# Cluster one-hots on GpSimd and ScalarE, mask rows by transfers, and another order of preparation in an attention and MoE kernel

## The chip, the cores and the metric

The kernel runs on one core of a Trainium2 chip. The metric is the device time of one execution in microseconds (us). TensorE (PE in the profile) multiplies and transposes; VectorE (DVE), ScalarE (ACT) and GpSimd (POOL) compute; SyncE (SP) and GpSimd issue the transfers. Each engine runs its instructions in the order in which the program gives them, and a waiting instruction holds up all behind it.

## What is computed

Clustered attention (2 batches, 8 heads, 768 positions, 64 features), then two MoE layers on its 1536 x 512 result. The change lies in the attention alone.

```python
q_assign = np.argmax(np.einsum('bhsd,hcd->bhsc', q_n, c_n), axis=-1)   # 16 clusters a head
k_assign = np.argmax(np.einsum('bhsd,hcd->bhsc', k_n, c_n), axis=-1)
mask = q_assign[:, :, :, None] == k_assign[:, :, None, :]
scores = np.where(mask, scale * np.matmul(q, k.transpose(0, 1, 3, 2)), -1000000000.0)
attn = np.exp(scores - np.max(scores, axis=-1, keepdims=True))
attn = attn / (np.sum(attn, axis=-1, keepdims=True) + 1e-09)
# x = attn @ v, then a gated MoE (512 -> 1536 -> 512) and a 4-expert MoE (512 -> 1024 -> 512)
```

## The kernel before

**Heads and slots.** There are 16 head instances g (2 batches x 8 heads). A unit u is half of a head's queries (384 rows), a slot is 128 query rows, so a unit has 3 slots, a head 6, and a pair of heads (p) 12; 96 slots in all, preceded by 5 slots of lead. The program is in an order written out by hand. In each slot the engines get, in the order "ESTLAtVMlvZB" (L549): the exponential of one score tile (E, `s_exp`, ScalarE), the score matmuls of the tile five slots ahead (S, `s_mm`, TensorE), three transposes of the probabilities (T, `transp`), with a copy "hi" by ScalarE (L347), VectorE's subtraction "lo" for the previous one (L, `low`, L361), the tasks of position a, the value matmuls (V, `pv`), three more transposes (t), the row maximum (M, `s_max`, L324, VectorE), then l, v, and the tasks of positions z and b. So "-9b" in a list of steps means: the last place of the ninth slot before a base slot.

**Scores with a mask.** A score tile is two products summed in PSUM: `t1` (hi and low halves of q and k, 128 rows) and `t2` (64 rows of the other combination, and in rows 64 to 79 the one-hot of the query's cluster and, for the keys, (one-hot - 1) x 2^60). A key of another cluster so gets a huge negative score. Each is done as two halves of 384 keys, in two banks of PSUM (L315 to L319).

**Clusters.** `cluster(g)` (L244) is a generator whose steps are spread over slots: 12 matmuls against the centroids (L259), a ScalarE copy and a VectorE addition (L266, L268), the maximum over 16 clusters (L270), equality with the maximum (L272), a product with tie weights (L274), a second maximum (L275), the one-hot (L277), six TensorE transposes (L283), and four ScalarE operations that write 16 rows of `t2` (L298, L300). Head 0 has its own form (L287 to L290). The lists CL, CL1, CL2 and CL4 (L518 to L521) place the steps.

**Operands.** `load_qk(g)` (L211) brings `t1` and `t2` by GpSimd's queue and the raw halves by SP's; `rest_qk(g)` subtracts the low halves on GpSimd (L226). Heads 0 and 1 come instead by `load_raw`, with the casts `hi_raw`, `hi_t2` and the subtraction `low_raw` by ScalarE and VectorE. `load_v`, `rest_v` (L240, GpSimd) bring the values.

**Pairs.** `recip(p)` makes the reciprocals of the row sums and spreads them by SP transfers: rT to DRAM (`rd`, L415), then R (L418). `pv_out` copies the result and, at the end of a pair, issues three SP transfers x (L394 to L396). `norm(p)` scales on GpSimd (L427, L432, L438) with ScalarE copies (L436).

Of the kernel before, what the change touches and what calls it, by code (L numbers as in the profile page):

```python
# [18 lines left out]
NCL = 16  # L19
# [7 lines left out]
BIG = float(2.0 ** 60)  # L27
F64_LO = 2.0 ** -126
# [7 lines left out]
def tile_cluster_attention_moe(ctx, tc, qk, vt, cent, consts, wm1, wm2, probs, out):  # L36
# [137 lines left out]
    def attention():  # L174
        with ExitStack() as ax:
# [27 lines left out]
            def low_raw(g, j):  # L203
                r = slice(64, 128) if j == 0 else slice(0, 64)
                t = ops[g]["t1"][r, j]
                V.tensor_tensor(out=t, in0=ops[g]["raw"][j][r], in1=t.bitcast(F32), op=ALU.subtract)
# [37 lines left out]
            def cluster(g):  # L244


                N = 2 * NQ
                t1, t2 = ops[g]["t1"], ops[g]["t2"]
                oh = oh_t[g % 2]
                ohn = oh[:, :, :, :NCL]  # L250
                pc = (ps_v if g == 1 else ps_c).tile([128, N, 2, NCL], F32, tag="v" if g == 1 else "c", name="pc")
                sc = clp.tile([128, N, NCL], F32, tag="sc", name="sc", bufs=2)
                mx = clp.tile([128, N, 1], F32, tag="mx", name="mx", bufs=2)
                eq = clp.tile([128, N, NCL], BF16, tag="eq", name="eq", bufs=2)
                mw = clp.tile([128, N, 1], BF16, tag="mw", name="mw", bufs=2)
                wb = wtie.rearrange("p (o c) -> p o c", o=1).to_broadcast([128, N, NCL])
                for j in range(2):
                    for c in range(NQ):
                        T.matmul(  # L259
                            out=pc[:, 2 * c + j].rearrange("p a b -> p (a b)"),  # L260
                            lhsT=t1[:, j, c * 128:(c + 1) * 128],
                            rhs=cT[:, g % H].rearrange("p a b -> p (a b)"),
                            start=True, stop=True,
                        )
                    yield
                A.copy(out=sc, in_=pc[:, :, 1])  # L266
                yield
                V.tensor_tensor(out=sc, in0=pc[:, :, 0], in1=sc, op=ALU.add)  # L268
                yield
                V.tensor_reduce(out=mx, in_=sc, axis=AX.X, op=ALU.max)  # L270
                yield
                V.tensor_tensor(out=eq, in0=sc, in1=mx.to_broadcast([128, N, NCL]), op=ALU.is_equal)  # L272
                yield
                V.tensor_tensor(out=eq, in0=eq, in1=wb, op=ALU.mult)  # L274
                V.tensor_reduce(out=mw, in_=eq, axis=AX.X, op=ALU.max)  # L275
                yield
                V.tensor_tensor(  # L277
                    out=ohn, in0=eq.rearrange("p (c j) n -> p c j n", j=2),
                    in1=mw.rearrange("p (c j) n -> p c j n", j=2).to_broadcast([128, NQ, 2, NCL]), op=ALU.is_equal)
                yield  # L280
                pt = ps_t.tile([64, S], BF16, tag="t", name="pt") if g == 0 else ps_c.tile([64, S], BF16, tag="c", name="pt")
                for c in range(NQ):
                    T.transpose(pt[:, c * 128:(c + 1) * 128], oh[:, c].rearrange("p j n -> p (j n)"), identb)  # L283
                yield
                if g == 0:
                    hs = [slice(i * 384, (i + 1) * 384) for i in range(2)]
                    A.activation(out=t2[64:80, 1, hs[0]], in_=pt[32:48, hs[0]], func=ACTF.Copy, scale=BIG, bias=-BIG)  # L287
                    V.tensor_scalar(out=t2[64:80, 1, hs[1]], in0=pt[32:48, hs[1]], scalar1=1.0, scalar2=BIG, op0=ALU.subtract, op1=ALU.mult)
                    for i in range(2):
                        A.copy(out=t2[64:80, 0, hs[i]], in_=pt[0:16, hs[i]])  # L290
                    yield
                else:
                    for j in range(2):
                        for i in range(2):
                            hs = slice(i * 384, (i + 1) * 384)
                            dst, src = t2[64:80, j, hs], pt[j * 32:j * 32 + 16, hs]
                            if j == 0:
                                A.copy(out=dst, in_=src)  # L298
                            else:
                                A.activation(out=dst, in_=src, func=ACTF.Copy, scale=BIG, bias=-BIG)  # L300
                            yield
# [7 lines left out]
            def s_mm(n):  # L309
# [5 lines left out]
                for c in range(2):  # L315
                    ps = S_t[n][:, c, :384]
                    ks = slice(c * 384, (c + 1) * 384)
# [3 lines left out]
            def s_max(n):  # L321
# [3 lines left out]
                    out=junk.rearrange("p (c n) -> p c n", c=2), in0=S_t[n][:, :, :384],  # L325
                    in1=zero1.rearrange("p (o n) -> p o n", o=1).to_broadcast([128, 2, 384]), scale=-0.125, scalar=3.0e38,
                    op0=ALU.add, op1=ALU.min, accum_out=nm)

            def s_exp(n):
# [6 lines left out]
                A.activation(out=P_t[n].rearrange("p (c n) -> p c n", c=2), in_=S_t.pop(n)[:, :, :384], func=ACTF.Exp, scale=0.125, bias=nm_t.pop(n),  # L336
# [126 lines left out]
            V.memset(zero1, 0.0)  # L463

# [10 lines left out]
            load_raw(1)  # L475
            setup, head = consts_setup(clp, ps_c), cluster(0)
# [3 lines left out]
            hi_raw(0, 0, A.copy)  # L480
            next(setup)
            low_raw(0, 0)
# [5 lines left out]
            low_raw(0, 1)  # L488
# [4 lines left out]
            load_qk(2)  # L493
# [3 lines left out]
            for j in range(2):  # L497
                hi_raw(1, j, A.copy)
            for _ in range(5):
                next(head)  # L500
            warm(8)
            low_raw(1, 0)
            next(head)
            next(head)
            low_raw(1, 1)
            for j in range(2):
                hi_t2(1, j, A.copy)
# [7 lines left out]
            for p in range(P - 1):  # L515
                steps(12 * (p + 1), ("1a", "2z", "2b"), recip(p))
                steps(12 * (p + 1), ("7a", "7b", "8a", "8z", "10a"), norm(p, G))
            CL = ("-18z", "-16a", "-16a", "-16z", "-15z", "-14a", "-12a", "-9a", "-9b", "-9b", "-8z", "-7b", "-7z")  # L518
            CL1 = ("-4a", "-4z", "-3a", "-3a", "-3z", "-2a", "-2z", "-1a", "-1z", "-1b", "0z", "0b")
            CL2 = ("-12z", "-12b", "-11a", "-11z", "-11b", "-10z", "-10b", "-9a", "-9b", "-9b", "-8z", "-7z", "-7b")  # L520
            CL4 = ("-16a", "-16z", "-16b", "-15a", "-15z", "-14a", "-12a", "-9a", "-9b", "-9b", "-8z", "-7z", "-7b")  # L521
            steps(0, CL1, head)
            LQ = {3: -3, 4: 2}
            RQ = {2: ("-13z", "-13b"), 3: ("-15b", "-13b"), 4: ("-19b", "-17b")}
            for g in range(NH):
                c = 6 * g
                if g > 2:
                    at(LQ.get(g, c - 23), "z", lambda g=g: load_qk(g))
                if g > 1:
                    steps(c, RQ.get(g, ("-22b", "-20b")), lazy(rest_qk, g, G))  # L530
                    steps(c, {2: CL2, 3: CL2, 4: CL4}.get(g, CL), lazy(cluster, g))
# [411 lines left out]
```

## Time and profile before

| What | Value |
|---|---|
| time, median of 3 runs | 1084.88 us (1079.38 to 1085.52) |
| time of the profiled execution | 1080.05 us |
| its span, first to last instruction | 1078.3 us |
| busy TensorE, VectorE, ScalarE, GpSimd | 1054.8, 717.7, 470.2, 178.1 us |
| granted TensorE clock, mean | 0.993 |

The busy times are over the whole span. Attention takes the first quarter or so, the MoE layers the rest, and the engines share the work differently in the two. Matmuls overlap and their ends are modelled, so a busy TensorE need not be at its peak.

### The profile page before, as it was taken

What the parts mean: (1) busy time and instruction counts of PE and PEld (TensorE: products, weight loads), DVE (VectorE), ACT (ScalarE), POOL (GpSimd) and SP (SyncE); (2) the same over time, 40 slices, a digit from 0 to 9 for tenths busy, and PEclk for the clock granted to TensorE, in tenths of its full rate; (3) what the DMA queues carried; (4) which work ended last, traced back from release to release, by engine and by line L of the source; (5) the groups of instructions that cost most, each with busy time, mean ns of one, the idle gap of its engine ahead of it and who ended that gap; (6) DMA issues with size and microseconds to landing.
All of it is one profiled execution on the core that took longest, in us unless ns stands there. A gap on an engine that the chain in (4) does not pass through costs nothing.

```text
span 1078.3 us, 13732 instructions
## 1 busy us (share of the span) xinstructions
PE 1054.8 (98%) x5193; PEld 873.3 (81%) x5193; DVE 717.7 (67%) x1245; ACT 470.2 (44%) x939; POOL 178.1 (17%) x178
## 2 busy tenths in 40 slices
PE   7999999999999999999999999999999999999998
PEld 5888878787788888888888888888888888888887
DVE  7798989998566555646748556665555656555554
ACT  6688888888544134314424222223331222333121
POOL 4435565442000000000101011111001111110100
PEclk9999999999999999999999999999999999999999
DMA  9656757731122222212301010111101011110003
GB/s 235 158 139 150 180 131 176 173 75 43 36 78 78 60 62 61 92 40 60 96 1 40 20 40 20 40 40 40 40 20 40 20 40 40 40 40 30 30 1 118
DMA packets 34467, 75.99 MB, mean 70 GB/s; under 512 B 12352, under 2 KB 16928, under 8 KB 34400
## 3 DMA queue, kind: packets, MB, share of 16 engines
q1 hardware_dynamic: 22528, 56.41, 17.9%
q0 software_dynamic: 11584, 18.62, 7.9%
q8 instruction: 41, 0.67, 0.3%
q14 instruction: 26, 0.21, 0.1%
q10 hardware_dynamic: 288, 0.07, 0.0%
HBM read 67.76 MB, written 3.19 MB: 66 GB/s over the span
## 4 chain that ended last, share of the span: by engine, by line
PE 91%; DVE 7%; ACT 1%; issue 1%; DMA 0%; SPq 0%; ACTq 0%; DVEq 0%
PE pd L876 24%; PE pb L163 17%; PE pa L746 12%; PE pd L843 9%; PE pa L163 9%; PE ps L342 5%; PE ps L318 2%; PE ps L319 2%; PE pb L746 2%; DVE junk L324 2%; PE pv L372 2%; PE pv L377 2%; PE pv L378 2%; DVE lo L361 2%; PE pc L259 2%; PE pu L163 1%
## 5 line engine op out<-in xcount | busy, mean ns | idle before, releaser
L883 DVE SCALAR_TENSOR_TENSOR acc<-pd,pn,acc 128x512 f32<-128x512 f32 (+1 forms) x181 | 133.9, 746 | 89.5 <-PE pd L876 89.5
L876 PE MATMUL pd<-wdh,hh 128*128 128x512 f32 (+1 forms) x386 | 149.7, 388 | 0.0
L876 PE MATMUL pd<-wdh,hl 128*128 128x512 f32 (+1 forms) x386 | 149.7, 388 | 0.0
L876 PE MATMUL pd<-wdl,hh 128*128 128x512 f32 (+1 forms) x386 | 149.7, 388 | 0.0
L754 ACT COPY snap<-pa 128x512 f32<-128x512 f32 x48 | 28.2, 588 | 265.2 <-PE pa L746 265.2
L134 POOL TENSOR_TENSOR ws<-wraw 128x256 f32<-128x256 f32 x16 | 12.3, 766 | 672.1 <-DMA wraw<-in_wm 543.5
L163 PE MATMUL pb<-xh,wuh 128*128 128x512 f32 x264 | 102.7, 389 | 0.0
L163 PE MATMUL pb<-xl,wuh 128*128 128x512 f32 x264 | 102.7, 389 | 0.0
L163 PE MATMUL pb<-xh,wul 128*128 128x512 f32 x264 | 102.7, 389 | 0.0
L324 DVE CUSTOM_DVE_ANT_1 junk<-ps,zero 128x768 bf16<-128x768 f32 x96 | 91.1, 949 | 14.7 <-PE ps L319 13.8
L342 PE MATMUL ps<-ident,P 128*128 128x128 f32 x576 | 88.4, 281 | 12.2 <-DVE lo L361 11.2
L336 ACT ACTIVATE P<-ps,nm 128x768 f32<-128x768 f32 x96 | 87.0, 906 | 7.8 <-DVE nm L324 6.2
L342 PEld LDWEIGHTS ps<-ident,P 128*128 128x128 f32 x576 | 67.7, 142 | 26.3 <-DVE lo L361 18.3
L876 PEld LDWEIGHTS pd<-wdh,hl 128*128 128x128 f32 x386 | 72.5, 188 | 15.0
L876 PEld LDWEIGHTS pd<-wdl,hh 128*128 128x128 f32 x386 | 72.5, 188 | 14.9
L876 PEld LDWEIGHTS pd<-wdh,hh 128*128 128x128 f32 x386 | 72.5, 188 | 14.9
L361 DVE TENSOR_TENSOR lo<-ps,hi 128x384 fp32r<-128x384 f32 x128 | 67.5, 550 | 8.9 <-ACT hi L347 8.6
L318 PE MATMUL ps<-t 80*128 80x384 f32 x192 | 70.3, 366 | 1.2 <-ACT t L290 0.9
L319 PE MATMUL ps<-t 128*128 128x384 f32 x192 | 66.0, 344 | 0.0
L347 ACT CAST hi<-ps 128x384 fp32r<-128x384 f32 x128 | 56.3, 482 | 20.9 <-PE ps L342 20.0
L759 ACT ACTIVATE hh<-sg 128x512 fp32r<-128x512 f32 x48 | 30.3, 632 | 72.3 <-DVE sg L766 72.3
L226 POOL TENSOR_TENSOR t<-raw,t 64x768 fp32r<-64x768 f32 x28 | 51.3, 1832 | 60.1 <-DMA raw<-in_qk 41.7
(171 smaller groups left out, 2326.7 us busy)
## 6 DMA issues: line engine op xcount, KB each, us to landing
wraw<-in_wm SPq DMA_DIRECT2D x68, 512.0 KB, 3.5
t<-in_qk POOLq DMA_DIRECT2D x14, 768.0 KB, 5.7
raw<-in_qk SPq DMA_DIRECT2D x28, 192.0 KB, 5.5
t<-in_qk POOLq DMA_DIRECT2D x14, 384.0 KB, 6.9
x<-x SPq DMA_DIRECT2D x21, 192.0 KB, 6.2
R<-rd SPq DMA_DIRECT2D x16, 192.0 KB, 3.3
out<-acc SPq DMA_DIRECT2D x11, 256.0 KB, 2.0
vraw<-in_vt SPq DMA_DIRECT2D x16, 128.0 KB, 3.9
```

What stands on the lines that cost most here:

```text
L163: T.matmul(out=ps, lhsT=w[:, o:o + 128], rhs=x, start=(k == 0 and m == 0), stop=(k == 3 and m == 2))
L318: T.matmul(out=ps, lhsT=t2[:, 0, qs], rhs=t2[:, 1, ks], start=True, stop=False)
L319: T.matmul(out=ps, lhsT=t1[:, 0, qs], rhs=t1[:, 1, ks], start=False, stop=True)
L324: V.tensor_tensor_reduce(out=junk.rearrange("p (c n) -> p c n", c=2), in0=S_t[n][:, :, :384], in1=zero1.rearrange("p (o n) -> p o n", o=1) ...
L336: A.activation(out=P_t[n].rearrange("p (c n) -> p c n", c=2), in_=S_t.pop(n)[:, :, :384], func=ACTF.Exp, scale=0.125, bias=nm_t.pop(n), ac ...
L342: T.transpose(ps[:, i * 128:(i + 1) * 128], P_t[3 * u + i][:, j * 128:(j + 1) * 128], ident)
L347: A.copy(out=hi, in_=ps)
L361: V.tensor_tensor(out=lo, in0=ps, in1=hi.bitcast(F32), op=ALU.subtract)
L746: T.matmul(out=ps, lhsT=w[:, o:o + 128], rhs=r, start=first and i == 0 and m == 0, stop=i == 1 and m == 2, skip_group_check=not first)
L843: T.matmul(out=ps, lhsT=w[:, o:o + 128], rhs=x[:, f, sl], start=(n == 0), stop=(n == len(terms) - 1))
L876: T.matmul(out=ps, lhsT=x[:, f, ts_], rhs=w[:, f * DM + cs.start:f * DM + cs.stop], start=(f == 0 and m == 0), stop=(f == FC - 1 and m == 2))
L883: V.scalar_tensor_tensor(out=y, in0=ps, scalar=pe, in1=y, op0=ALU.mult, op1=ALU.add)
```

## The change

It does the following.

- For heads 3 to 15 the one-hot is made differently: GpSimd subtracts the maximum from the cluster scores, ScalarE multiplies by 2^120, GpSimd adds the tie weights, VectorE takes the maximum, GpSimd subtracts it, and ScalarE writes Relu(x + 1) as the one-hot. Heads 0 to 2 keep VectorE's form.
- The mask rows of heads 1 to 15 are made by one ScalarE operation from the transposed one-hots (64 x 768, scale and bias per row from `mkc`) into a tile `mk`, and two SP transfers put 16 rows each into `t2`. Head 0 uses three ScalarE operations.
- Head 2 comes by `load_raw`, as heads 0 and 1 do; its low halves are GpSimd's. Head 3 is loaded ahead of the first slot, behind a second gate.
- The scores are done as 512 and 256 keys, contiguous over one and a half banks.
- The steps of the clusters, of `rest_qk` and of `norm` move to other slots; some warm-up matmuls go.

```diff
--- before.py
+++ after.py
@@ -25,6 +25,7 @@
 NQ = S // 128
 NPAIR = H // 2
 BIG = float(2.0 ** 60)
+HUGE = float(2.0 ** 120)
 F64_LO = 2.0 ** -126
 F64_HI = 2.0 ** -96 * (1 + 0x6FF000 / 2.0 ** 23)
 FC = 2
@@ -200,10 +201,10 @@
             def hi_raw(g, j, copy):
                 copy(out=ops[g]["t1"][:, j], in_=ops[g]["raw"][j])
 
-            def low_raw(g, j):
+            def low_raw(g, j, eng):
                 r = slice(64, 128) if j == 0 else slice(0, 64)
                 t = ops[g]["t1"][r, j]
-                V.tensor_tensor(out=t, in0=ops[g]["raw"][j][r], in1=t.bitcast(F32), op=ALU.subtract)
+                eng.tensor_tensor(out=t, in0=ops[g]["raw"][j][r], in1=t.bitcast(F32), op=ALU.subtract)
 
             def hi_t2(g, j, copy):
                 copy(out=ops[g]["t2"][0:64, j], in_=ops[g]["raw"][j][0:64])
@@ -249,7 +250,7 @@
                 oh = oh_t[g % 2]
                 ohn = oh[:, :, :, :NCL]
                 pc = (ps_v if g == 1 else ps_c).tile([128, N, 2, NCL], F32, tag="v" if g == 1 else "c", name="pc")
-                sc = clp.tile([128, N, NCL], F32, tag="sc", name="sc", bufs=2)
+                sc = clp.tile([128, N, NCL], F32, tag="sc", name="sc")
                 mx = clp.tile([128, N, 1], F32, tag="mx", name="mx", bufs=2)
                 eq = clp.tile([128, N, NCL], BF16, tag="eq", name="eq", bufs=2)
                 mw = clp.tile([128, N, 1], BF16, tag="mw", name="mw", bufs=2)
@@ -269,36 +270,43 @@
                 yield
                 V.tensor_reduce(out=mx, in_=sc, axis=AX.X, op=ALU.max)
                 yield
-                V.tensor_tensor(out=eq, in0=sc, in1=mx.to_broadcast([128, N, NCL]), op=ALU.is_equal)
-                yield
-                V.tensor_tensor(out=eq, in0=eq, in1=wb, op=ALU.mult)
-                V.tensor_reduce(out=mw, in_=eq, axis=AX.X, op=ALU.max)
-                yield
-                V.tensor_tensor(
-                    out=ohn, in0=eq.rearrange("p (c j) n -> p c j n", j=2),
-                    in1=mw.rearrange("p (c j) n -> p c j n", j=2).to_broadcast([128, NQ, 2, NCL]), op=ALU.is_equal)
+                if g < 3:
+                    V.tensor_tensor(out=eq, in0=sc, in1=mx.to_broadcast([128, N, NCL]), op=ALU.is_equal)
+                    V.tensor_tensor(out=eq, in0=eq, in1=wb, op=ALU.mult)
+                    yield
+                    V.tensor_reduce(out=mw, in_=eq, axis=AX.X, op=ALU.max)
+                    yield
+                    V.tensor_tensor(
+                        out=ohn, in0=eq.rearrange("p (c j) n -> p c j n", j=2),
+                        in1=mw.rearrange("p (c j) n -> p c j n", j=2).to_broadcast([128, NQ, 2, NCL]), op=ALU.is_equal)
+                else:
+                    G.tensor_tensor(out=sc, in0=sc, in1=mx.to_broadcast([128, N, NCL]), op=ALU.subtract)
+                    yield
+                    A.activation(out=sc, in_=sc, func=ACTF.Copy, scale=HUGE)
+                    yield
+                    G.tensor_tensor(out=sc, in0=sc, in1=wb, op=ALU.add)
+                    yield
+                    V.tensor_reduce(out=mx, in_=sc, axis=AX.X, op=ALU.max)
+                    yield
+                    G.tensor_tensor(out=sc, in0=sc, in1=mx.to_broadcast([128, N, NCL]), op=ALU.subtract)
+                    yield
+                    A.activation(out=ohn, in_=sc.rearrange("p (c j) n -> p c j n", j=2), func=ACTF.Relu, bias=1.0)
                 yield
                 pt = ps_t.tile([64, S], BF16, tag="t", name="pt") if g == 0 else ps_c.tile([64, S], BF16, tag="c", name="pt")
                 for c in range(NQ):
                     T.transpose(pt[:, c * 128:(c + 1) * 128], oh[:, c].rearrange("p j n -> p (j n)"), identb)
                 yield
                 if g == 0:
-                    hs = [slice(i * 384, (i + 1) * 384) for i in range(2)]
-                    A.activation(out=t2[64:80, 1, hs[0]], in_=pt[32:48, hs[0]], func=ACTF.Copy, scale=BIG, bias=-BIG)
-                    V.tensor_scalar(out=t2[64:80, 1, hs[1]], in0=pt[32:48, hs[1]], scalar1=1.0, scalar2=BIG, op0=ALU.subtract, op1=ALU.mult)
-                    for i in range(2):
-                        A.copy(out=t2[64:80, 0, hs[i]], in_=pt[0:16, hs[i]])
+                    A.activation(out=t2[64:80, 1], in_=pt[32:48], func=ACTF.Copy, scale=BIG, bias=-BIG)
+                    for hs in (slice(0, 384), slice(384, S)):
+                        A.copy(out=t2[64:80, 0, hs], in_=pt[0:16, hs])
                     yield
                 else:
+                    mk = clp.tile([64, S], F32, tag="mk", name="mk")
+                    A.activation(out=mk, in_=pt, func=ACTF.Identity, scale=mkc[:, 0:1], bias=mkc[:, 1:2])
                     for j in range(2):
-                        for i in range(2):
-                            hs = slice(i * 384, (i + 1) * 384)
-                            dst, src = t2[64:80, j, hs], pt[j * 32:j * 32 + 16, hs]
-                            if j == 0:
-                                A.copy(out=dst, in_=src)
-                            else:
-                                A.activation(out=dst, in_=src, func=ACTF.Copy, scale=BIG, bias=-BIG)
-                            yield
+                        SY.dma_start(out=t2[64:80, j].bitcast(F32), in_=mk[32 * j:32 * j + 16])
+                    yield
 
             P_t, rs_t, nm_t, pT, pv_t, xu_t, r_t = {}, {}, {}, {}, {}, {}, {}
 
@@ -312,9 +320,9 @@
                 t1, t2 = ops[g]["t1"], ops[g]["t2"]
                 qs = slice(half * 384 + i * 128, half * 384 + i * 128 + 128)
                 S_t[n] = ps_s.tile([128, 2, 512], F32, tag="s", name="ps")
-                for c in range(2):
-                    ps = S_t[n][:, c, :384]
-                    ks = slice(c * 384, (c + 1) * 384)
+                S_t[n] = S_t[n].rearrange("p c n -> p (c n)")[:, :S]
+                for ks in (slice(0, 512), slice(512, S)):
+                    ps = S_t[n][:, ks]
                     T.matmul(out=ps, lhsT=t2[:, 0, qs], rhs=t2[:, 1, ks], start=True, stop=False)
                     T.matmul(out=ps, lhsT=t1[:, 0, qs], rhs=t1[:, 1, ks], start=False, stop=True)
 
@@ -322,8 +330,7 @@
                 junk = sm.tile([128, S], BF16, tag="junk", name="junk", bufs=1)
                 nm = nm_t[n] = sm.tile([128, 1], F32, tag="nm", name="nm", bufs=4)
                 V.tensor_tensor_reduce(
-                    out=junk.rearrange("p (c n) -> p c n", c=2), in0=S_t[n][:, :, :384],
-                    in1=zero1.rearrange("p (o n) -> p o n", o=1).to_broadcast([128, 2, 384]), scale=-0.125, scalar=3.0e38,
+                    out=junk, in0=S_t[n], in1=zero1.to_broadcast([128, S]), scale=-0.125, scalar=3.0e38,
                     op0=ALU.add, op1=ALU.min, accum_out=nm)
 
             def s_exp(n):
@@ -333,7 +340,7 @@
                     rs_t[p] = sm.tile([128, 2, NQ], F32, tag="rs", name="rs")
                 c = half * 3 + i
                 P_t[n] = pp.tile([128, S], F32, tag="P", name="P")
-                A.activation(out=P_t[n].rearrange("p (c n) -> p c n", c=2), in_=S_t.pop(n)[:, :, :384], func=ACTF.Exp, scale=0.125, bias=nm_t.pop(n),
+                A.activation(out=P_t[n], in_=S_t.pop(n), func=ACTF.Exp, scale=0.125, bias=nm_t.pop(n),
                              accum_out=rs_t[p][:, h, c:c + 1])
 
             def transp(u, j):
@@ -461,6 +468,9 @@
             for h in range(2):
                 V.memset(oh_t[h], 0.0)
             V.memset(zero1, 0.0)
+            mkc = clp.tile([64, 2], F32, name="mkc")
+            for j, v in enumerate((1.0, 0.0, BIG, -BIG)):
+                V.memset(mkc[j // 2 * 32:j // 2 * 32 + 32, j % 2:j % 2 + 1], v)
 
             def warm(n):
 
@@ -473,38 +483,46 @@
             load_raw(0)
             consts_load(clp, A, ("ident", "wt"))
             load_raw(1)
+            load_raw(2)
             setup, head = consts_setup(clp, ps_c), cluster(0)
             warm(11)
             next(setup)
             next(setup)
             hi_raw(0, 0, A.copy)
+            low_raw(0, 0, V)
             next(setup)
-            low_raw(0, 0)
             warm(3)
             next(head)
             hi_raw(0, 1, A.copy)
             A.copy(out=gate, in_=ops[0]["raw"][1][:, 0:1])
             G.memset(gate, 0.0)
-            low_raw(0, 1)
+            low_raw(0, 1, V)
             next(head)
             warm(5)
             next(setup, None)
             load_v(0)
-            load_qk(2)
             for j in range(2):
                 hi_t2(0, j, V.tensor_copy)
             next(head)
             for j in range(2):
                 hi_raw(1, j, A.copy)
+            A.copy(out=gate, in_=ops[1]["raw"][1][:, 0:1])
+            G.memset(gate, 0.0)
+            load_qk(3)
+            for j in range(2):
+                hi_raw(2, j, A.copy)
             for _ in range(5):
                 next(head)
-            warm(8)
-            low_raw(1, 0)
+            warm(4)
+            low_raw(1, 0, V)
             next(head)
+            hi_t2(1, 0, V.tensor_copy)
             next(head)
-            low_raw(1, 1)
+            low_raw(1, 1, V)
+            hi_t2(1, 1, V.tensor_copy)
             for j in range(2):
-                hi_t2(1, j, A.copy)
+                hi_t2(2, j, A.copy)
+                at(-4 + j, "z", lambda j=j: low_raw(2, j, G))
             head = cluster(1)
             next(head)
             for i in range(5):
@@ -514,21 +532,19 @@
             steps(NS, ("-5z", "-4a", "-4z"), recip(P - 1))
             for p in range(P - 1):
                 steps(12 * (p + 1), ("1a", "2z", "2b"), recip(p))
-                steps(12 * (p + 1), ("7a", "7b", "8a", "8z", "10a"), norm(p, G))
-            CL = ("-18z", "-16a", "-16a", "-16z", "-15z", "-14a", "-12a", "-9a", "-9b", "-9b", "-8z", "-7b", "-7z")
-            CL1 = ("-4a", "-4z", "-3a", "-3a", "-3z", "-2a", "-2z", "-1a", "-1z", "-1b", "0z", "0b")
-            CL2 = ("-12z", "-12b", "-11a", "-11z", "-11b", "-10z", "-10b", "-9a", "-9b", "-9b", "-8z", "-7z", "-7b")
-            CL4 = ("-16a", "-16z", "-16b", "-15a", "-15z", "-14a", "-12a", "-9a", "-9b", "-9b", "-8z", "-7z", "-7b")
-            steps(0, CL1, head)
-            LQ = {3: -3, 4: 2}
-            RQ = {2: ("-13z", "-13b"), 3: ("-15b", "-13b"), 4: ("-19b", "-17b")}
+                steps(12 * (p + 1), ("8b", "9z", "10a", "10z", "11z"), norm(p, G))
+            CL = ("-14z", "-13a", "-13a", "-13z", "-12z", "-12b", "-11a", "-11a", "-10a", "-10a", "-9a", "-9b", "-9b")
+            CL1 = ("2a", "2z", "3a", "3a", "3z", "4a", "4z", "5a", "5z")
+            CL2 = ("-12z", "-12b", "-11a", "-11z", "-11b", "-10a", "-10b", "-9a", "-9b", "-9b")
+            steps(-6, CL1, head)
             for g in range(NH):
                 c = 6 * g
+                if g > 3:
+                    at(c - 23, "z", lambda g=g: load_qk(g))
                 if g > 2:
-                    at(LQ.get(g, c - 23), "z", lambda g=g: load_qk(g))
+                    steps(c, ("-19b", "-15a") if g % 2 else ("-19b", "-15b"), lazy(rest_qk, g, G))
                 if g > 1:
-                    steps(c, RQ.get(g, ("-22b", "-20b")), lazy(rest_qk, g, G))
-                    steps(c, {2: CL2, 3: CL2, 4: CL4}.get(g, CL), lazy(cluster, g))
+                    steps(c, CL2 if g == 2 else CL, lazy(cluster, g))
                 if g:
                     at(c - 8, "z", lambda g=g: load_v(g))
                 at(c - 4, "z", lambda g=g: rest_v(g))
```

## Rows read from the trace of the kernel before

**Rows 1.** Windows: us; busy us of PE, PEld, DVE, ACT, POOL; clock; DMA share, GB/s.

```profile
28.96:227.50 198.54, 188.07 (x1237) 159.63 (x1236) 180.76 (x371) 165.44 (x375) 102.66 (x86) 0.97 0.65 150
242.20:256.88 14.68, 14.01 (x95) 11.83 (x94) 13.05 (x27) 13.76 (x32) 3.30 (x3) 1.00 0.15 28
84.00:88.00 4.00, 4.00 (x19) 3.18 (x19) 2.76 (x8) 1.93 (x4) 1.90 (x2) 0.59 0.51 83
290.00:1070.00 780.00, 780.00 (x3442) 645.85 (x3442) 468.04 (x726) 240.37 (x425) 48.13 (x64) 1.00 0.14 45
```

**Rows 2.** The chain of waits, TensorE: start us, us, what.

```profile
22.27 0.52 PE pt L283 x6
...
207.40 0.17 PE pv L377
...
208.10 0.18 PE ps L318
...
208.81 0.66 PE ps L342 x6
209.46 0.80 PE pv L372 x4
210.26 0.77 PE pc L259 x6
```

**Rows 3.** Who waited for whom, 28.96 to 227.5: us, times, longest.

```profile
PEld ps L342 <- DVE lo L361: 15.4, 30, 2.2
```

**Rows 4.** Groups of instructions of VectorE, 28.96 to 227.5: busy us, mean ns, idle before.

```profile
L272 DVE TENSOR_TENSOR eq<-sc,mx 128x192 bf16<-128x192 f32 x13 | 14.0, 1079 | 0.0
...
L274 DVE TENSOR_TENSOR eq<-eq,wtie 128x192 bf16<-128x192 bf16 x13 | 10.1, 777 | 0.1
L277 DVE TENSOR_TENSOR oh<-eq,mw 128x192 bf16<-128x192 bf16 x12 | 9.8, 813 | 0.0
...
L275 DVE TENSOR_REDUCE mw<-eq 128x12 bf16<-128x192 bf16 x13 | 4.6, 353 | 0.4
```

**Rows 5.** Timeline, VectorE and GpSimd: start us, us, engine, line, operation, tiles.

```profile
33.21 0.35 DVE L272 TENSOR_TENSOR eq<-sc,mx 128x192 bf16<-128x192 f32 x1
33.60 0.26 DVE L274 TENSOR_TENSOR eq<-eq,wtie 128x192 bf16<-128x192 bf16 x1
...
218.56 1.83 POOL L226 TENSOR_TENSOR t<-raw,t 64x768 fp32r<-64x768 f32 x1 [3.67 <-DMA t<-in_qk]
218.91 1.70 DVE L272 TENSOR_TENSOR eq<-sc,mx 128x192 bf16<-128x192 f32 x1
```

**Rows 6.** Groups of instructions of ScalarE, 28.96 to 227.5.

```profile
L336 ACT ACTIVATE P<-ps,nm 128x768 f32<-128x768 f32 x72 | 65.2, 906 | 5.4 <-DVE nm L324 4.2
...
L298 ACT CAST t<-pt 16x384 fp32r<-16x384 bf16 x24 | 11.2, 468 | 1.7 <-PE pt L283 1.2
...
L266 ACT COPY sc<-pc 128x192 f32<-128x192 f32 x13 | 4.2, 323 | 1.9 <-PE pc L259 1.7
```

**Rows 7.** Groups of instructions of GpSimd, 28.96 to 227.5.

```profile
L240 POOL TENSOR_TENSOR vs<-vraw,vs 128x256 fp32r<-128x256 f32 x12 | 9.7, 807 | 2.4 <-DMA vs<-in_vt 2.4
```

**Rows 8.** Timeline: SP's transfers of one pair, and a row maximum.

```profile
101.29 0.33 SPq L415 DMA_DIRECT2D rd<-rT  x1
104.59 1.09 SPq L418 DMA_DIRECT2D R<-rd  x2
...
112.54 0.96 DVE L324 CUSTOM_DVE_ANT_1 junk<-ps,zero 128x768 bf16<-128x768 f32 x1 [0.38 <-PE ps L319]
```

**Rows 9.** DMA issues of the page: KB each, median us from issue to landing.

```profile
x<-x SPq DMA_DIRECT2D x21, 192.0 KB, 6.2
R<-rd SPq DMA_DIRECT2D x16, 192.0 KB, 3.3
```

**Rows 10.** Timeline, ScalarE and TensorE, where cluster 2 begins.

```profile
25.69 0.85 ACT L300 ACTIVATE t<-pt 16x384 fp32r<-16x384 bf16 x2
26.64 1.04 PE L259 MATMUL pc<-cT,t 128*128 128x32 f32 x8 [1.89 <-issue]
```

## The prediction

> **What bounds the kernel now.** I read the table by stretches first. From 290 us on, the MoE keeps TensorE busy 780.00 of 780.00 us [rows 1]: nothing of the change touches it, so the change is worth what it moves the end of attention, which lies before. Between 28.96 us (the row maximum of slot 1) and 227.50 us (that of slot 73) lie 72 of the 96 slots, twelve heads of six slots, at 198.54 / 12 = 16.55 us a head [rows 1]. VectorE is busy 180.76 us there, 15.06 us a head, ScalarE 165.44, 13.79 a head, GpSimd 102.66 [rows 1].
>
> TensorE looks busy too, but its ends are modelled, so I take its own work from the chain of waits, where consecutive pieces give the spacing. A 384-column matmul takes about 0.175 us (four from 207.40 to 208.10), six transposes 0.66, the four last-value matmuls of a unit 0.80, six cluster matmuls 0.77 [rows 2]; six one-hot transposes take 0.52 [rows 2]. A unit of three slots has 12 score matmuls (2.10), 18 transposes (1.98), 8 value matmuls (1.40) and the 0.80: 6.28 us. Two units make a head, 12.56, and a cluster adds 2 x 0.77 + 0.52 = 2.06: 14.6 us. So 16.55 - 14.6 = 1.95 us a head, 23.4 us over the twelve, is TensorE waiting or slowed. The waits say for whom: the weight loads of the attention transposes wait 15.4 us for VectorE's subtraction "lo", L361 [rows 3]. VectorE is in order; L361 stands behind the cluster's operations. Part of the 23.4 is clock: in 84 to 88 us the granted clock was 0.59, on average between TensorE's two levels, 1.2 and 2.4 GHz [rows 1], (1 - 0.59) x 4 = 1.6 us lost.
>
> Why VectorE is late: L272, L274 and L277 take 1.079, 0.777 and 0.813 us on average [rows 4], but 0.35, 0.26 and, by the same shape as L272, about 0.35 when GpSimd is idle [rows 4, 5]. At 218.91 us L272 took 1.70; GpSimd's L226 ran from 218.56 for 1.83 [rows 5], and L272 ended 0.2 us after it. Some 0.73 x 13 + 0.52 x 13 + 0.46 x 12 = 21.8 us of VectorE's stretch is this blocking, near the 23.4.
>
> **The change, part by part.**
>
> *One-hots of heads 3 to 15.* VectorE loses 1.079 + 0.777 + 0.813 = 2.67 us a head, to 12.4; the maximum L275, 0.353, is exchanged for one over as many float elements [rows 4]. GpSimd gains three operations of 128x192. Nearest row: L240, 128x256 in 0.807 [rows 7]; by elements 0.61 each, 1.8 a head, some 20 us over eleven heads, so 123 of about 184 us. No row has a broadcast or a mixed-type GpSimd operand; bounds 0.5 and 1.83 (the 768-element L226 [rows 5]); I take 0.61, being the nearest shape. ScalarE gains two 128x192 operations (0.323, as L266) and one 64x768 one (0.906, as the exponential of the same length), and loses four of 0.47 [rows 6]: -0.33 us, 13.46 a head.
>
> What speaks against it: the last stretch of the first table, 242.20 to 256.88, has no cluster matmuls, VectorE 13.05 and ScalarE 13.76 busy, and takes 14.68 [rows 1], although TensorE's sum there is only 12.56 + 0.52 = 13.1. With ScalarE 94% busy, 1.6 us of waiting stays. So TensorE does not fall to its 14.6. After the change ScalarE is no lighter than there (13.46 against 13.76) and VectorE slightly lighter (12.4 against 13.05). I take 15.3 us a head: less than half of the 1.6 on top of 14.6, because the longer TensorE work covers part of it. Gain 1.25 x 12 = 15 us. Bounds: 0 (ScalarE takes VectorE's place) and 23.4.
>
> The Trainium skill, page "SBUF — State Buffer", section "Who interferes with whom", says that a VectorE instruction with two SBUF inputs and a GpSimd instruction that reads SBUF exclude each other for the whole instruction. The rows of L272 and L226 above agree. By it the three L-operations stop being blocked, and the new GpSimd operations can block only what still has two SBUF inputs.
>
> *New waits.* ScalarE, in order, now waits for GpSimd twice a head (scaling at -11a, Relu at -9a), with the exponentials and "hi" copies behind it, and TensorE behind those. At pair borders GpSimd has, from 11z on, L438 and the first half of rest_qk (1.83 each) and the first subtraction (0.61): 4.3 us, due 1.3 slots later, 1.3 x 2.55 = 3.3 us. So ScalarE is held about 1.0 us for each of 6 pairs, 6 us at most; the other borders have only one 1.83 ahead. I take 2 us. If the GpSimd operations take 1.83, it is 4.3 + 1.2 and another 7 us.
>
> *Mask rows.* One ScalarE operation, then two SP transfers of 48 KB, issued at slot -9b, read by the score matmul at -5. For even heads they queue behind recip's R. R's first issue was 3.3 us after rd's (101.29 to 104.59), 1.09 for the two [rows 8]; R lands 3.3 after its issue [rows 9]. Masks land 3.3 + 1.09 + 1.0 (two issues) + 3.3 = 8.7 us after rd. They are needed by head 6's first scores, whose row maximum began at 112.54 [rows 8], 11.25 us after rd; less 0.7 for the matmuls, and shortened by 15.3 / 16.55, 9.8 us. Hidden with 1.1 us to spare. If they land like the x copies, 6.2 [rows 9], they are 1.8 us late on six heads, 11 us. Bounds 0 and +11; I take +1, being nearer to R, which goes the same queue just before.
>
> *Scores 512 + 256.* 3442 matmuls of the MoE in 780.00 us give 0.227 for 512 columns [rows 1]; 256 columns lie between 0.117 (by proportion of 0.175) and 0.14 (midway between 0.11 of a 128-column transpose and 0.175). A slot's four cost 0.69 to 0.73 against 0.70: -1.2 to +3.2 us over 96 slots. I take +1. VectorE and ScalarE read the same 768 elements: 0.
>
> *Head 2 by plain loads, later loads, new slots.* Four head-2 casts join ScalarE before its first exponential; the transfer total falls (two of 384 KB instead of 1.5 MB). Work on SP, ScalarE and VectorE ahead of the first score is a microsecond more or less: bounds -1 to +2, I take 0. At 24.75 us TensorE idled 1.89 us until head 1's last mask copy (25.69 + 0.85) freed the bank for cluster 2 [rows 10]. The mask now comes a slot earlier; but head 1's scores then wait for its transfers. Bounds -1.9 to +3; I take -1. rest_qk moved from -22b to -19b/-15b: GpSimd no longer stands waiting for the load, which keeps its queue open for the new operations; no gain by itself, and at 2.55 us a slot the low halves are ready two slots before their matmul at -14z / -13a. Later slots for norm: its xh halves are needed only by the MoE.
>
> Sum: -15 + 2 + 1 + 1 + 0 - 1 = -12 us, 1080.05 - 12 = 1068. The profiled execution (span 1078.3) lies 4.8 us under the median shown, 1084.88, and within its runs; I keep 1068 as the median of after.
>
> **The rivals.**
>
> *ScalarE takes over.* For: 13.46 us a head busy, three engines in line, and 94% at 14.68 [rows 1]. Against: VectorE's 2.68 us are real, and the waits name L361. A head stays at 16.2: gain 4, less the 3 of the other terms: about 1079, no change.
>
> *The masks, or GpSimd, come too late (slower).* ScalarE held by GpSimd is the mechanism, at -11a. GpSimd falls behind when its operations cost near 1.83: then it has 102.66 + 11 x 5.5 = 163 us of 184, and in pair borders a queue of 5.5 us against 3.3. It decides once ScalarE is held over 1.5 us in each of 13 heads at both places: 13 x 2 x 1.5 = 39, less the 15: 1104. Against: three rows of GpSimd go by elements, 1.83 for 768, 0.807 for 256.
>
> *Offloading gives nothing, since the port is shared.* The remaining VectorE operations with two SBUF inputs in the stretch, the weight steps, are fewer than 20; each blocked once by 0.61: 12 us at most, and the gain shrinks from 15 to 3: 1080. Against: L361 and the row maxima, on which TensorE and ScalarE wait, are not among them. The page "Perfetto Trace Analysis", section "Optimizing Scalar/DVE Operations", warns that moving work between these two engines might not help for this reason.
>
> *All of it.* TensorE falls to 14.6: -23.4 - 1.9 - 1.2 = -26.5, with the clock never dropping: 1053.
>
> **How the numbers follow.** Forecast (1059 to 1074) 0.52; all of it (1050 to 1059) 0.14; ScalarE takes over, the port, or masks as late as the x copies (1074 to 1086) 0.24: 0.14, 0.04 and 0.06; GpSimd late (1090 to 1110) 0.10. The range 1052 to 1086 leaves out the last and a few per cent below. One per cent, 10.8 us, is about what a measurement of this kernel can tell from no change: faster than 1074, 0.66; within, 0.24; slower, 0.10.
>
> **What would show it.** Right: heads of about 15.3 us between the same row maxima, L361 hardly named in TensorE's waits, VectorE near 12.4 a head, GpSimd's new operations near 0.6 us, no stretch at a lower granted clock. Wrong: ScalarE waiting for GpSimd at the scaling or the Relu, score matmuls waiting for a transfer into t2, GpSimd operations over 1 us, or a head above 16.

## The result, and the profile after

The change makes the kernel slower: 1093.0 us, median of six runs (1088.98 to 1093.72), against 1082.16 for the kernel before in six runs beside it (1079.38 to 1085.52). The ratio is 1.0083, 95% interval 1.0058 to 1.0107. Against the forecast of 1068 that is 25 us, and it lies outside the range of 1052 to 1086.

The table by stretches of after, columns as in [rows 1]: the twelve heads from the 7th row maximum to the 79th, two stretches within them, and the MoE.

```profile
35.42:239.59 204.17, 187.79 (x1233) 157.89 (x1232) 159.52 (x335) 157.19 (x360) 114.95 (x116) 0.92 0.66 152
172.00:176.00 4.00, 1.96 (x14) 1.51 (x12) 4.00 (x5) 1.83 (x5) 3.53 (x4) 0.92 1.13 323
176.00:180.00 4.00, 4.00 (x21) 2.54 (x20) 1.71 (x5) 2.45 (x4) 1.79 (x1) 0.59 0.82 73
310.00:1080.00 770.00, 770.00 (x3399) 637.55 (x3398) 461.86 (x716) 236.24 (x419) 48.36 (x64) 0.95 0.14 44
```

The MoE did not change: 770.00 / 3399 is 0.2265 us a matmul, 0.2266 before [rows 1]. (The clock is recorded as 0.95 there, but the spacing is that of before, so I read 0.95 as this recording's full level.) The span grew from 1078.3 to 1090.9 us, by 12.6, all of it in attention. The 7th row maximum moved from 28.96 to 35.42, 6.5 us; the twelve heads take 204.17 us instead of 198.54 [rows 1], 5.6 us more; 0.5 us comes after them. VectorE did get lighter there, 159.52 us against 180.76: 13.3 us a head, not 12.4.

By the row maxima the twelve heads take from 15.13 us (the one that begins with slot 12) to 18.94, on average 17.01; in before they take from 15.22 to 18.39. The two heads behind the twelve take 15.32 and 15.19 us, in before 14.70 and 14.68. So undisturbed heads did not become clearly shorter, and the long ones come from few places. The largest, in the timeline of after (start, duration, engine, line, tiles; in brackets the wait before):

```profile
171.81 0.54 POOL L291 TENSOR_TENSOR sc<-sc,mx 128x192 f32<-128x192 f32 x1
172.14 2.95 DVE L118 TENSOR_SCALAR wa<-wa 128x512 f32<-128x512 f32 x1
172.29 0.75 POOL L241 TENSOR_TENSOR vs<-vraw,vs 128x256 fp32r<-128x256 f32 x1
172.99 1.81 POOL L227 TENSOR_TENSOR t<-raw,t 64x768 fp32r<-64x768 f32 x1
175.01 0.55 DVE L362 COPY pT<-ps 128x384 f32<-128x384 f32 x1
175.61 0.75 PE L349 MATMUL ps<-ident,P 128*128 128x128 f32 x3 [2.04 <-DVE pT L362]
```

L118 is a weight step with one SBUF input. It stands still while GpSimd finishes one operation and runs two more behind it, and ends 0.3 us after the last. TensorE waits behind it for the copy L362, and in the next stretch above its granted clock is 0.59, on average between the two levels of 1.2 and 2.4 GHz. VectorE and TensorE are held in the same way at 71 us (L118, 2.94 us) and 105 us (L126, 2.86 us), but there TensorE goes on at full speed (0.95, this recording's full level, from 72 to 78 and from 106 to 112 us).

TensorE's other large wait, again from the timeline of after, is for the mask rows of heads 1 and 12 (a third, for head 4, is 1.0 us; SPq is the issue of a transfer on SP):

```profile
27.69 1.22 SPq L308 DMA_DIRECT2D t<-mk  x2
28.95 0.59 SPq L218 DMA_DIRECT2D raw<-in_qk  x1
33.76 0.77 PE L326 MATMUL ps<-t 80*128 80x512 f32 x1 [3.87 <-DMA t<-mk]
...
208.46 0.32 SPq L422 DMA_DIRECT2D rd<-rT  x1
214.74 1.09 SPq L425 DMA_DIRECT2D R<-rd  x2
215.93 1.09 SPq L89 DMA_DIRECT2D wraw<-in_wm  x1
217.12 1.18 SPq L308 DMA_DIRECT2D t<-mk  x2
222.12 0.48 PE L326 MATMUL ps<-t 80*128 80x512 f32 x1 [2.59 <-DMA t<-mk]
```

Together, in the table of waits between 10 and 290 us (who waited for whom: sum, times, longest):

```profile
POOL sc L287 <- ACT sc L285: 21.2, 13, 3.9
PEld ps L349 <- DVE lo L368: 8.8, 13, 1.9
PEld ps L349 <- DVE pT L362: 7.9, 5, 2.6
PE ps L326 <- DMA t<-mk: 7.5, 3, 3.9
```

In the same window of before the weight loads wait 18.3 us for "lo" (15.4 over the twelve heads [rows 3]), here 8.8: it fell, as meant. Their wait for the copy pT, behind a blocked weight step, grew from 1.3 us to 7.9, and the wait for the masks is new. GpSimd waits for ScalarE; ScalarE for GpSimd does not occur.

### The profile page after: what moved, and what is told of

It is laid out like the page before. It is cut to its first block, busy times and chain, and to the rows that moved or that the text cites. A ratio compares the mean times of both kernels' runs of the same rounds, so it can differ in the third digit from the quotient of the medians.

```text
span 1090.9 us, 13855 instructions
## 1 busy us (share of the span) xinstructions
PE 1058.1 (97%) x5189; PEld 873.5 (80%) x5189; DVE 697.9 (64%) x1211; ACT 462.1 (42%) x923; POOL 197.3 (18%) x216
## 4 chain that ended last, share of the span: by engine, by line
PE 90%; ACT 3%; DVE 3%; issue 2%; DMA 2%; SPq 0%; ACTq 0%; DVEq 0%
PE pd L892 24%; PE pb L164 16%; PE pa L762 12%; PE pd L859 9%; PE pa L164 8%; PE ps L349 5%; PE ps L326 3%; PE ps L327 2%; PE pv L379 2%; PE pb L762 2%; PE pv L384 2%; PE pv L385 2%; PE pc L260 2%; DMA t<-mk 1%; PE pu L164 1%
## 5 line engine op out<-in xcount | busy, mean ns | idle before, releaser
L326 PE MATMUL ps<-t 80*128 80x512 f32 x192 | 73.8, 385 | 10.6 <-DMA t<-mk 7.5
L368 DVE TENSOR_TENSOR lo<-ps,hi 128x384 fp32r<-128x384 f32 x128 | 69.4, 554 | 13.8 <-ACT hi L354 12.6
L327 PE MATMUL ps<-t 128*128 128x512 f32 x192 | 63.9, 352 | 0.0
L326 PEld LDWEIGHTS ps<-t 80*128 80x128 f32 x192 | 38.3, 199 | 28.1 <-ACT hi L354 8.1
```

The lines of the kernel that those rows point to most:

```text
L326: T.matmul(out=ps, lhsT=t2[:, 0, qs], rhs=t2[:, 1, ks], start=True, stop=False)
L327: T.matmul(out=ps, lhsT=t1[:, 0, qs], rhs=t1[:, 1, ks], start=False, stop=True)
L368: V.tensor_tensor(out=lo, in0=ps, in1=hi.bitcast(F32), op=ALU.subtract)
```

## The experiments

All are given as ratios to the kernel before, measured beside them, with 95% intervals. Each has one trace, and starts differ from trace to trace: in two kernels with the same first slots (the combined ones below) the first row maximum came at 15.06 and 16.81 us.

### The start: head 1's casts on ScalarE, head 2's later

```diff
-            hi_t2(1, 0, V.tensor_copy)
+            hi_t2(1, 0, A.copy)
...
-            hi_t2(1, 1, V.tensor_copy)
+            hi_t2(1, 1, A.copy)
...
-                hi_t2(2, j, A.copy)
+                at(-3 + j, "z", lambda j=j: hi_t2(2, j, A.copy))
```

> Only the start differs from the changed kernel (1093.0 us): the two t2 casts of head 1 go back from VectorE to ScalarE, and the two t2 casts of head 2 go to slots -3 and -2. Theory A (VectorE's casts took 2.05 and 2.15 us instead of 0.5 because GpSimd's subtractions for head 2 ran at the same time, and the first row maximum stood behind them): the first row maximum begins near 16 us instead of 18.4, and the time falls by 2 to 4 us, to 1089 to 1091. Rival B (the first scores are late for another reason, or head 1's wait for its mask transfer takes the gain back): under 1 us, 1092 to 1094.

Measured: 1.0063 (1.0042 to 1.0085). What it is meant to take away, in the timeline of after (L210 are the two casts that go to ScalarE):

```profile
12.53 2.03 POOL L207 TENSOR_TENSOR t<-rawqk,t 64x768 fp32r<-64x768 f32 x1
12.92 2.05 DVE L210 CAST t<-rawqk 64x768 fp32r<-64x768 f32 x1
15.53 2.51 POOL L207 TENSOR_TENSOR t<-rawqk,t 64x768 fp32r<-64x768 f32 x1
16.30 2.15 DVE L210 CAST t<-rawqk 64x768 fp32r<-64x768 f32 x1
18.38 0.94 DVE L332 CUSTOM_DVE_ANT_0 junk<-ps,zero 128x768 bf16<-128x768 f32 x1
```

In the trace of before two such casts together took 0.98; here each takes two, beside GpSimd's new low halves of head 2, and the first row maximum waits behind them, at 18.38 instead of 16.10. With the casts on ScalarE it came at 17.02, but the 7th still at 35.34: head 1's mask wait took the gain back. The interval overlaps after's: the 2 us less that the ratio gives are not told apart from nothing, and the trace speaks for rival B.

### The weight steps in slots without GpSimd's run

```diff
-            WA, WB = ("0b", "2b", "7a", "7z"), ("2z", "7b", "7b")
+            WA, WB = ("0b", "4b", "7a", "7z"), ("4b", "7b", "7b")
```

> Only two slots differ from the changed kernel: the weight steps at 2b and 2z of the pairs go to 4b. Theory A (VectorE's weight operations at 12p+2 stand blocked behind a run of GpSimd operations, 2.86 to 2.95 us instead of 0.4 to 0.7, three times, and TensorE waits 2.0 to 2.3 us each time and then runs at the lower clock for some microseconds): no weight operation over 1.5 us, and 6 to 11 us less, 1082 to 1087. Rival B (the GpSimd runs are wherever GpSimd is, and block another operation instead, or the wait is taken back by the PE-bound slots behind it): within 2 us of 1093.

Only the steps at 2b and 2z move; those at 0b and 7 stay. Measured: 0.9989 (0.9968 to 1.0010), 0.94% below after, and the intervals don't meet. The weight steps of this kernel's twelve heads, these heads in its table by stretches, and the same two steps in before (there L125 and L117):

```profile
L126 DVE TENSOR_TENSOR wul<-wa,wuh 128x512 fp32r<-128x512 f32 x3 | 2.1, 693 | 3.0 <-ACT wuh L125 3.0
L118 DVE TENSOR_SCALAR wa<-wa 128x512 f32<-128x512 f32 x4 | 1.9, 469 | 0.1
...
35.47:231.92 196.45, 183.75 (x1233) 155.45 (x1232) 152.69 (x335) 156.74 (x360) 114.28 (x116) 0.98 0.68 158
...
L117 DVE TENSOR_SCALAR wa<-wa 128x512 f32<-128x512 f32 x4 | 2.3, 575 | 0.1
L125 DVE TENSOR_TENSOR wul<-wa,wuh 128x512 fp32r<-128x512 f32 x3 | 2.1, 693 | 2.9 <-ACT wuh L124 2.9
```

In after L118 took 1726 ns on average and L126 1415, in before 575 and 693: the long blocking came with the change. VectorE loses 6.8 us of busy time, the heads 7.7 us of 204.17. The mean clocks can't be set side by side as recorded: 0.92 in after is of a full level of 0.95, that is 0.97 of full, as in before [rows 1], and here it is 0.98. This is the largest of the causes that were tested.

### The one-hots on VectorE again

```diff
-                if g < 3:
+                if True:
```

> The one-hots of heads 3 to 15 are made by VectorE again, in the slots of the changed kernel; all else as changed. Theory A (moving the one-hots is a gain of its own, hidden by stalls of the start, the weight steps and the mask transfers): slower than the changed kernel by 5 to 15 us, 1098 to 1108, with VectorE's equality and product again near 0.8 to 1.1 us. Rival C (the one-hots on GpSimd and ScalarE are themselves the loss: the scaling and the Relu stand between ScalarE's copies, and GpSimd holds the port): faster by 4 us or more, under 1089.

Measured: 1.0406 (1.0367 to 1.0446), 3.2% above after, some 34 us where 5 to 15 were expected. VectorE's one-hot lines there, from 30 to 280 us (count, busy, mean ns, wait before):

```profile
L275 DVE TENSOR_TENSOR eq<-eq,wtie 128x192 bf16<-128x192 bf16 x13 | 18.6, 1434 | 0.4
L274 DVE TENSOR_TENSOR eq<-sc,mx 128x192 bf16<-128x192 f32 x13 | 9.1, 697 | 0.4
L279 DVE TENSOR_TENSOR oh<-eq,mw 128x192 bf16<-128x192 bf16 x13 | 9.0, 696 | 0.4
```

So VectorE's form costs in these slots. It doesn't price the move from before's slots: the new ones lie closer together, and not all else is as in after. VectorE's form has three steps fewer, the list of slots is filled from its start, and so transposes and masks come earlier (ScalarE's mask operation of head 3 in slot 13, in after in slot 14). How much of the 3.2% is the form and how much the slots is not shown.

### Head 1's mask rows by ScalarE, straight from PSUM

```diff
+                elif g == 1:
+                    A.activation(out=t2[64:80, 1], in_=pt[32:48], func=ACTF.Copy, scale=BIG, bias=-BIG)
+                    A.copy(out=t2[64:80, 0], in_=pt[0:16])
+                    yield
```

> Only head 1's mask rows differ from the changed kernel: two ScalarE operations write them straight from PSUM, without transfers. Theory A (head 1's scores wait 3.87 us for the two transfers, which are in flight together with 1.5 MB of head 4, and TensorE then runs at the lower clock): no wait for a mask transfer at head 1, 4 to 6 us less, 1087 to 1089. Rival B (head 1's scores are late anyway, by the cluster matmuls of head 2 and the start): under 1.5 us.

Measured: 1.0056 (1.0032 to 1.0081); it overlaps after's. The trace is plain: the 7th row maximum came at 29.68 instead of 35.42, and the 91st at 265.21 instead of 270.10. Head 12's wait stayed, 3.38 us.

### All masks that way

The same two ScalarE operations for all heads from 1 on, in place of `mk` and the transfers.

> The mask rows of all heads are written by two ScalarE operations straight from PSUM; no mask transfers; else the changed kernel. Theory A (only head 1 and one or two even heads wait for transfers; elsewhere the transfers are hidden and save ScalarE some 0.6 us a head): 4 to 8 us less than 1093.0, about what head 1 alone gave, 1085 to 1089. Rival B (the transfers delay every head through SP's queue): 10 us less or more, under 1083. Rival C (ScalarE is the limit between the PE-bound slots, so 0.6 us a head more of it costs): no gain over head 1 alone, 1088 to 1094.

Measured: 1.0050 (1.0029 to 1.0071), as with head 1 alone. No score matmul waits for a transfer any more, but the slot in which ScalarE copies takes 3.24 and 3.56 us, where it was 2.71 to 2.76 in after. The transfers do relieve ScalarE, about as much as their late landings cost: rival C.

### Scores as 384 + 384

> The scores again as two halves of 384 keys; else the changed kernel. Both theories say that the split costs next to nothing (four matmuls in 0.71 us against 0.70): 1091 to 1095. A change of 4 us or more would show that the row maximum or the exponential pays for the shape.

Measured: 1.0065 (1.0041 to 1.0089), not told apart from after. The four matmuls of a slot take 0.23 + 0.23 + 0.12 + 0.12 us in after, about 0.70; the term of +1 us was at most that.

### Start, head 1's mask and weight steps together

The edits of the first, second and fourth experiment together.

> The three edits that each took one suspected stall away (the head 1 casts on ScalarE, the weight steps at 4b, head 1's mask rows by ScalarE operations), together on the changed kernel. Measured alone they gave -2.6, -11.2 and -5.0 us against 1093.0. Theory A (separate stalls one after another in time): the sum or a little more, since the start's gain is no longer taken back at head 1's mask: 1070 to 1076, below the kernel before. Rival B (each is followed by a wait that the other hides): about that of the weight steps alone, 1079 to 1083.

Measured: 0.9946 (0.9924 to 0.9968). Against after the three alone give -0.20, -0.94 and -0.27, together -1.41%; measured -1.37%. Within the intervals they add up; that the start has a part in it is not shown, since without it the sum is -1.21%. But head 4's masks now came late, TensorE waiting 3.1 us for them; SP's issues in the timeline of this kernel:

```profile
64.83 0.39 SPq L426 DMA_DIRECT2D rd<-rT  x1
72.32 1.09 SPq L429 DMA_DIRECT2D R<-rd  x2
73.50 1.19 SPq L312 DMA_DIRECT2D t<-mk  x2
```

R can be issued only when rd has landed, here 7.5 us later, and the masks stand behind it on the same queue.

### The same, with recip's transfers behind the masks

```diff
                 A.copy(out=rT, in_=ps)
+                yield
                 rd = dram.tile([2 * NQ, 128], F32, tag="rd", name="rd")
...
-                steps(12 * (p + 1), ("1a", "2z", "2b"), recip(p))
+                steps(12 * (p + 1), ("1a", "2z", "2b", "4a"), recip(p))
```

(The last pair's list gets one step more as well.)

> As the kernel with the three edits, and in recip the two transfers that spread the reciprocals go to 4a, behind the even heads' mask transfers instead of ahead of them on SP's queue. Theory A (the mask waits of 1.3 to 3.4 us that stay at heads 6, 8 or 12 come from the masks queued on SP behind R, which itself waits for rd): no wait for a mask transfer, 2 to 5 us less than that kernel. Rival B (masks are late because ScalarE writes them late, or the transfers land late): the same waits, within 1 us.

Measured: 0.9874 (0.9846 to 0.9903), 1071.66 us: the fastest, faster than before as well, and its interval lies below that of the kernel without this edit. Its timeline on SP and its heads:

```profile
70.48 1.19 SPq L312 DMA_DIRECT2D t<-mk  x2
71.72 0.59 SPq L427 DMA_DIRECT2D rd<-rT  x1
76.27 1.13 SPq L430 DMA_DIRECT2D R<-rd  x2
...
30.86:221.32 190.46, 181.74 (x1233) 153.27 (x1232) 153.50 (x336) 156.55 (x362) 116.58 (x118) 0.99 0.71 167
```

No score matmul waits for a mask; 190.46 / 12 is 15.87 us a head. One weight step is still blocked, L126 at 103 us, 1.94 us long beside GpSimd's L227, and TensorE waits 1.2 us for the "lo" behind it.

### That edit alone

> Only recip differs from the changed kernel: its two transfer steps go to 4a, so that even heads' masks no longer stand behind R on SP's queue. Theory A (head 12's scores wait 2.6 us for a mask queued behind R and a weight load, 8.7 us after rd's issue, and TensorE then runs at the lower clock): no mask wait but head 1's, 3 to 5 us less, 1088 to 1090. Rival B (in the changed kernel only one even head waits, so it matters only once the other stalls are gone and the slots are shorter): under 2 us, 1091 to 1094.

Measured: 1.0064 (1.0041 to 1.0088), overlapping after's. Of the mask waits only head 1's is left (4.03 us). The weight steps are still blocked, 2.94, 2.86 and 2.94 us: while the slots are that long, few other masks are late, and the 2 us less that the ratio gives are not told apart from nothing.

### All weight steps in slots 3 and 4 as well

The fastest version, with the weight steps in slots 3 and 4 for every pair but the last, whose list stays as it is.

> As the fastest kernel so far (three edits and recip's transfers at 4a, 1071.7), with all weight steps of a pair in slots 3 and 4, none at 0b and 7. Theory A (a head is three slots of 2.7 us that TensorE sets, and three others that ScalarE's and VectorE's chain sets; weight steps cost only in the others): first slots of odd and even heads fall from 2.9 to 4.6 us towards 2 to 2.5, 3 to 7 us less, 1065 to 1069. Rival B (GpSimd's second half of rest_qk for odd heads runs in slot 3 and blocks the weight operations there; or the two slots become longer than 2.7): no gain or a loss, 1071 to 1076.

Measured: 0.9890 (0.9859 to 0.9920): no gain. Even heads fall to 14.85 to 14.89 us, but of the odd heads head 3 grows from 15.97 to 18.28, with L120 blocked for 2.20 beside GpSimd's L227, and head 13 from 14.53 to 19.17. The steps meet GpSimd elsewhere: rival B.

## Why the prediction was wrong

**What failed, and what held.** With four collisions taken away (the casts, the weight steps, head 1's mask, the order on SP's queue) the same one-hots give 1071.66 us, inside the forecast's band. That step from after is -2.09%, some 23 of the 25 us of the miss, so the failed step is the rest of the sum: it held nothing, or next to nothing, for these four.

The mechanism of the main term, VectorE late with "lo", was right in direction: that wait fell, and VectorE went from 15.06 us a head to 13.3, and to 12.7 with the weight steps moved (forecast 12.4). Its size is not confirmed. In the traces the heads of the fastest version average 15.87 us, 0.67 less than in before, where 1.25 was forecast: 8 of 15 us over the twelve. Its start is still 1.9 us later than before's (the 7th row maximum at 30.86 against 28.96). So that the time comes near 1068 is in part luck. No run has the four edits on the kernel before, or VectorE's one-hots in the fastest version; what the one-hots by themselves give is open.

**The port, as a rival.** The prediction saw that the weight steps could be blocked, priced them "each blocked once by 0.61: 12 us at most", and left this out of the sum, with a chance of 0.04. It counted only operations with two SBUF inputs. L118 has one, and was held through a run of GpSimd operations, 2.9 us instead of 0.47, TensorE waiting 2.0 to 2.3 us behind it each time (and once, at 176 us, with matmuls at twice their spacing after it). The counter-argument, that "lo" and the row maxima are not among the blocked, missed that VectorE works in order: L362 is not blocked, but stands behind. Measured: 0.94%, 10 us. That this is near the 12 is luck: not twenty operations blocked by 0.61, but three by some 2.4. The Trainium skill, page "SBUF — State Buffer", section "Who interferes with whom", lists cast and tensor_scalar among the operations that can take the pair of ports that VectorE shares with GpSimd, when their operands meet certain conditions, and says that the loser blocks for the whole instruction. So the prediction's "only what still has two SBUF inputs" was a misreading of that section. The casts and L118 agree; that the loser waits for several instructions in a row is what the trace adds.

**Head 1's mask.** "Bounds -1.9 to +3; I take -1": a freed bank and a transfer that hardly waits. The issue came at 27.69, with head 4's loads around it, and TensorE waited 3.87 us and then ran at half speed (three 384-column matmuls at 36.78, 37.10 and 37.42, 0.32 apart instead of about 0.175 [rows 2]); the 7th row maximum is 6.5 us later. About 5.7 of it goes with this transfer (35.42 to 29.68). The bound of +3 lacked the clock and the late landing. That head 4's loads make it late is likely, but no run takes them away.

**Head 2 and the start.** "A microsecond more or less" counted operations, not their neighbours: +2.3 us at the first row maximum, with the casts at two microseconds each. In time nothing of it was measured; behind the mask wait it could not show, and with the mask mended the 7th row maximum lies at 28.52, 30.86 and 29.71 with the casts moved, at 29.68 and 30.62 without, which doesn't tell them apart.

**Masks of even heads.** The step "R's first issue was 3.3 us after rd's" carried a row of before [rows 8] over into after. In before the interval is 4.5, 3.3, 2.8, 3.7, 2.8 and 1.3 us, so the row was a usual one; in after it is 7.7, 6.0, 4.9, 6.0, 6.3 and 1.3, and a weight load (L89) can stand between R and the masks. SP's waits up to 300 us, before and after:

```profile
SPq L418 <- DMA rd<-rT: 17.7, 8, 4.0
SPq L425 <- DMA rd<-rT: 31.5, 8, 7.2
```

What differs ahead of rd at the first five pairs is the load of the next head's `t` on GpSimd's queue: the first of its two transfers is issued 7.2 to 7.8 us ahead of rd in before, 2.1 to 2.9 in after. That these loads hold up rd's landing is argued, not shown by an edit. With heads of 15.3 us there are 9.8 us from rd to need, and by the 8.7 I had 1.1 to spare; in the kernel with the three edits together five mask waits came to 6.3 us. Reordered: -0.72%, 8 us (against the same kernel without).

**The others.** ScalarE waiting for GpSimd, +2 and the mechanism of the slower rival, was nothing: GpSimd's operations took 542, 552 and 520 ns, below the 0.61, and the table of waits has no such row. The slower side came from elsewhere. TensorE's 14.6 us, to which a head was not to fall, is reached: two heads of the fastest version take 14.54 and 14.56. The slots of a head have different limits, so the sum over a head of one engine's work says little. In slots in the middle of a head, 2.69 to 2.76 us mostly, TensorE is busy throughout; in 21 of the 24 first and last slots of the fastest version's twelve heads VectorE is busy for 92% or more.

**What stays open.** The remaining 0.57 us a head of the fastest version (15.87 against 15.3) is not explained. The largest wait left is TensorE's for VectorE's "lo" (10.5 us of the weight loads' time), but which operation to move was not found; in the last experiment moving more weight steps brought nothing. What the one-hots gain from before's slots was not measured by itself.

## What to carry to other kernels

When work goes to GpSimd, look at each VectorE operation that will run beside it, also those with one input, and at what stands behind it in order; price it by the whole run of GpSimd operations. A transfer that replaces an engine's copy needs the queue written out: what is issued ahead of it, which of these waits for a landing, and which loads will be in flight then. An interval read from the old trace holds only while its neighbours stay: here 2.8 to 4.5 us became 4.9 to 7.7.

## What was not expected of the hardware

In all three cases of after VectorE did not get in between GpSimd operations that followed one another: 2.86 to 2.95 us for operations of 0.42 to 0.69. Of the 48 KB mask transfers, those of after whose landing the trace has took 2.1 to 4.6 us from issue; head 1's are not among them, and TensorE went on 6.1 us after the first one's issue (27.69 to 33.76). After some waits TensorE's matmuls stood twice as far apart for some us, at a granted clock of 0.59 on average in the stretch above, so that such a wait costs more than itself: after 3.87 us at 33.76, 2.04 us at 175.61 and 2.59 us at 222.12. After 2.05 us at 74.48 and 2.32 us at 108.52 they did not; the traces don't show what decides it.
